# Small reads of two weight matrices at the start of an attention and MoE kernel: 16 partitions in place of 128

## The chip, the cores and the metric

The kernel runs on one core of one Trainium2 chip. The metric is the device time of one execution in microseconds (us): the median of five runs for the kernel before, and comparisons with it for the others. A difference of 0.3% is 0.68 us here.

## The reference

The program computes sliding-window attention with a few sink tokens, and feeds its result through a two-layer network with a gated activation. Cut to what matters:

```python
# q, k, v: (4, 8, 768, 64); n_sink 4, window 128
scores = q @ k.T / sqrt(64)                       # per batch and head
keep = (key < n_sink) | ((0 <= query - key) & (query - key < window))
a = softmax(where(keep, scores, -1e9))
x = (a @ v).transpose(0, 2, 1, 3).reshape(3072, 512)
h = x @ w_in                                      # w_in: (512, 2048)
g = h * sigmoid(beta * h)
out = g @ w_out                                   # w_out: (2048, 512)
```

Inputs and output are float32.

## The kernel before, in words

The 3072 tokens are cut into eight half batches of 384 tokens. For each, the kernel loads q, k and v (lines 613 to 638), casts them to bf16, transposes q and k, computes the scores of blocks of 128 keys by 128 queries that the window touches, takes the exponential on ScalarE, masks, multiplies by v, and normalises. The 384 rows then go through `w_in` (line 910), the gated activation (lines 915 and 917) and `w_out` (line 931). Half batches 0 and 1 are transposed on TensorE (line 697), later ones by DMA transposes (line 734).

`w_in` and `w_out` come in as 16 loads of 512 KB each (`load_w`, lines 640 to 648), float32 into staging tiles `wst` or, for some, into a part of the tile `g` that is not yet in use; they are cast to bf16 by `cast_w`. A load of `w_in` takes 512 columns of 256 rows; a load of `w_out` takes 256 whole rows. On both sides a row index within a block of 128 is the partition.

All of these loads, the transposing DMAs and the stores are issued by SyncE, in one queue. The order of TensorE's work is a string written out by hand (`ORDER`), one letter for each group of matmuls. A planner with a cost for each operation then places the work of the other engines and SyncE's DMAs in time (`schedule`), and puts filler matmuls on a tile of ones where it expects TensorE to be idle during the first 48 us (`fillers`; they have line 1027 in the profile). All this happens when the kernel is built: on the chip each engine runs a fixed list of instructions, with waits on semaphores.

The small reads stand outside of the planner. `G.touch` holds two transfers (line 508), each of which reads four float32 numbers (16 bytes) from the head of many rows: of each of the 512 rows of `w_in`, and of each row in every second block of 128 rows of `w_out`. They land in the tile `seen`, which nothing reads. `emit` issues them on ScalarE's queue ahead of ScalarE's list (lines 385 and 386), and SyncE waits for their semaphore at the very end. The tile `seen` is the last one that is allocated in SBUF. The first instruction of ScalarE's own list is a small exponential that loads its table (line 596).

Of the kernel before, what the change touches and what calls it, by code (L numbers as in the profile page):

```python
# [5 lines left out]
F32 = mybir.dt.float32  # L6
# [10 lines left out]
NM = DF // 128  # L17
# [388 lines left out]
def bass_streamingllm_window__then__act_swish_beta_kernel(  # L406
# [31 lines left out]

    G = Graph()
    _program(nc, G, sb, ps, q, k, v, moe_w_in, moe_w_out, moe_beta, out)  # L440
    G.schedule(ORDER)
    G.resolve()
# [12 lines left out]
def _program(nc, G, sb, ps, q, k, v, w_in, w_out, beta, out):  # L455
# [48 lines left out]
    w_in_src = w_in.rearrange("(c p) f -> p c f", p=128)  # L504
    w_out_src = w_out.rearrange("(m p) n -> p m n", p=128)
    osb = sb("osb", (128, NOUT), F32, NOS)
    seen = sb("seen", (128, 12, 4), F32)
    G.touch = [(seen[:, 0:4, :], w_in_src[:, :, 0:4]), (seen[:, 4:12, :], w_out_src[:, 0:NM:2, 0:4])]
    P = ps("P", (128, 8, 512))

    def add(eng, fn, ns, r=(), w=(), x=(), dma=None, queue=470, ring=64, lag=0, after=()):
# [551 lines left out]
```

The softmax here doesn't subtract the row's maximum and nothing guards it: scores larger than these inputs give would overflow.

## Time and profile before

| What | Before |
|---|---|
| Median of 5 runs | 226.16 us (225.94 to 226.99) |
| The profiled execution | 226.16 us |
| Its span, first to last instruction | 224.4 us |
| Mean granted TensorE clock | 0.992 |
| TensorE busy (share of the span) | 216.1 us (96%) |
| VectorE busy | 141.4 us (63%) |
| ScalarE busy | 141.8 us (63%) |
| GpSimd busy | 67.0 us (30%) |
| DMA moved | 40.95 MB in 104741 packets |
| of it on ScalarE's queue (q10) | 0.02 MB in 1568 packets |

Times in the profile are counted from the first instruction of the program. PE is TensorE's matmuls, PEld its weight loads, DVE VectorE, ACT ScalarE, POOL GpSimd, SP SyncE; a q after an engine's name (SPq, ACTq) means its issuing of DMAs. L697 is line 697 of the kernel. In lists of instructions the columns are start, duration, engine, line, operation, out<-in, and in brackets how long the engine had been idle and what ended that. In tables by stage there are the stage and its length, the busy time of PE, PEld, DVE, ACT and POOL with the number of instructions, the granted TensorE clock, the mean share of the DMA engines that was busy (over 1 where packets overlap), and GB/s. The chain is the work that ended last, followed back from the end: at each step to what released it.

### The profile page before, as it was taken

The numbers are of one execution on the slowest core, as the hardware profiler recorded it, in microseconds if no ns is written. First come the engines' busy times: TensorE is split into PE (matmuls) and PEld (weight loads), VectorE is DVE, ScalarE is ACT, GpSimd is POOL, SyncE is SP. The second block draws the span as 40 slices with busy tenths as digits, with TensorE's granted clock in tenths as the row PEclk, the third lists the DMA queues.
The fourth block names the chain that finished last, engine by engine and source line by source line (L and its number), as shares of the span: only waits on it lengthen the run. The fifth ranks groups of instructions, "written<-read, shape, count | busy, mean of one in ns | idle before, by whom it ended". The sixth has DMA issues, their size and how long they took to land.

```text
span 224.4 us, 4463 instructions
## 1 busy us (share of the span) xinstructions
PE 216.1 (96%) x1699; PEld 120.0 (53%) x1720; DVE 141.4 (63%) x313; ACT 141.8 (63%) x257; POOL 67.0 (30%) x157
## 2 busy tenths in 40 slices
PE   8889999999999999999999999999999999999994
PEld 3446555555455546545554665455555556555443
DVE  1797999788767288839774579657362626455100
ACT  2595998134882877547788748678747756566221
POOL 7274345000362627352109510231436400000000
PEclk9988999999999999999999999999999999999999
DMA  7999989997999999999999999993133033101112
GB/s 160 266 337 374 356 200 352 343 245 138 219 220 213 223 200 243 183 253 219 209 242 180 217 215 236 258 235 96 47 85 82 0 85 83 47 4 47 47 47 93
DMA packets 104741, 40.95 MB, mean 182 GB/s; under 512 B 93312, under 2 KB 97680, under 8 KB 104720
## 3 DMA queue, kind: packets, MB, share of 16 engines
q1 hardware_dynamic: 103152, 40.65, 80.3%
q8 instruction: 13, 0.21, 0.4%
q10 hardware_dynamic: 1568, 0.02, 0.4%
q14 instruction: 8, 0.07, 0.1%
HBM read 27.30 MB, written 6.29 MB: 150 GB/s over the span
## 4 chain that ended last, share of the span: by engine, by line
PE 71%; DVE 10%; DMA 8%; SPq 6%; ACT 3%; issue 1%
PE P L931 31%; PE P L910 28%; DMA v_stage<-in_v_dram 5%; SPq L635 5%; PE P L861 4%; DVE g L917 4%; PE P L783 4%; DMA k_stage<-in_k_dram 3%; PE P L851 2%; DVE k L563 1%; ACT t L915 1%; SPq L891 1%; PE P L819 1%; PE P L1027 1%; DVE w_in L563 1%
## 5 line engine op out<-in xcount | busy, mean ns | idle before, releaser
L910 PE MATMUL P<-xT,w_in 128*128 128x384 bf16 x512 | 92.7, 326 | 0.0
L915 ACT ACTIVATE t<-P,hbeta 128x384 f32<-128x384 f32 x128 | 71.9, 587 | 31.5 <-PE P L910 24.6
L917 DVE SCALAR_TENSOR_TENSOR g<-t,P 128x384 bf16<-128x384 f32 x128 | 68.0, 549 | 35.5 <-ACT t L915 32.9
L931 PE MATMUL P<-w_out,g 128*128 128x512 bf16 (+2 forms) x379 | 88.9, 370 | 1.3 <-ACT t L915 0.2
L798 POOL TENSOR_SCALAR_AFFINE_SELECT E<-E 128x256 bf16<-128x256 bf16 (+1 forms) x109 | 53.0, 518 | 57.1 <-ACT E L792 57.0
L910 PEld LDWEIGHTS P<-xT,w_in 128*128 128x128 bf16 x512 | 48.4, 98 | 34.7 <-issue 0.8
L931 PEld LDWEIGHTS P<-w_out,g 128*128 128x128 bf16 x400 | 36.6, 98 | 36.9 <-issue 1.1
L792 ACT ACTIVATE E<-P 128x768 bf16<-128x768 f32 (+1 forms) x64 | 45.6, 760 | 14.9 <-PE P L783 14.6
L861 PE MATMUL P<-vaug,E 128*128 128x65 bf16 x352 | 19.1, 196 | 0.3 <-DVE vaug L563 0.2
L861 PEld LDWEIGHTS P<-vaug,E 128*128 128x128 bf16 x352 | 17.1, 100 | 3.6 <-ACT E L792 0.7
L558 ACT ACTIVATE osb<-P 128x512 f32<-128x512 f32 (+2 forms) x16 | 9.1, 571 | 15.2 <-PE P L931 15.1
L868 DVE TENSOR_TENSOR onorm<-P,rden 128x384 bf16<-128x384 f32 x32 | 17.5, 553 | 0.5
L783 PE MATMUL P<-qkT 64*128 64x128 bf16 (+1 forms) x256 | 16.7, 242 | 0.9 <-ACT E L792 0.4
L823 ACT ACTIVATE ES<-P 128x128 bf16<-128x128 f32 (+1 forms) x32 | 12.0, 390 | 7.0 <-PE P L819 7.0
L563 DVE CAST k<-k_stage 128x512 bf16<-128x512 f32 (+1 forms) x24 | 11.8, 491 | 5.6 <-DMA k_stage<-in_k_dram 5.6
L783 PEld LDWEIGHTS P<-qkT 64*128 64x128 bf16 x256 | 8.2, 94 | 12.3 <-issue 3.8
L563 DVE CAST q<-q_stage 128x512 bf16<-128x512 f32 (+1 forms) x19 | 9.3, 489 | 6.7 <-DMA q_stage<-in_q_dram 6.5
L851 PE MATMUL P<-vS,ES 128*128 128x130 bf16 x64 | 12.8, 223 | 0.6 <-DVE vS L686 0.4
L563 DVE CAST vaug<-v_stage 128x512 bf16<-128x512 f32 x18 | 8.0, 446 | 7.6 <-DMA v_stage<-in_v_dram 7.5
L725 POOL TENSOR_TENSOR kS<-qkT,headm 128x8 bf16<-128x8 bf16 x16 | 3.0, 212 | 32.6 <-DMA qkT<-k 28.9
L1027 PE MATMUL P<-ones 128*128 128x512 bf16 (+2 forms) x31 | 9.9, 449 | 1.1 <-POOL ones L569 1.1
L809 DVE TENSOR_TENSOR E<-E,maskS 128x512 bf16<-128x512 bf16 x16 | 8.2, 511 | 3.1 <-ACT E L792 3.0
(48 smaller groups left out, 87.9 us busy)
## 6 DMA issues: line engine op xcount, KB each, us to landing
v_stage<-in_v_dram SPq DMA_DIRECT2D x24, 256.0 KB, 4.6
out_dram<-osb SPq DMA_DIRECT2D x23, 256.0 KB, 2.6
q_stage<-in_q_dram SPq DMA_DIRECT2D x18, 256.0 KB, 4.6
k_stage<-in_k_dram SPq DMA_DIRECT2D x18, 256.0 KB, 5.7
wst<-in_moe_w_in_dram SPq DMA_DIRECT2D x5, 512.0 KB, 7.8
wst<-in_moe_w_out_dram SPq DMA_DIRECT2D x4, 512.0 KB, 8.0
g<-in_moe_w_out_dram SPq DMA_DIRECT2D x4, 512.0 KB, 6.8
q_stage<-in_q_dram SPq DMA_DIRECT2D x8, 192.0 KB, 4.6
```

Of the source, the lines that this page charges most:

```text
L563: return lambda e: e.tensor_copy(dst, at())
L783: add("pe", lambda e, dst=dst, own=own, kc=kc, rows=rows, q0=q0, nq=nq: e.matmul(dst(), tokens(own, hp, 1, rows, kc, 1)[:, 0, :], tokens(h ...
L792: add("act", lambda e, src=src, dst_=dst_: e.activation(dst_, src(), AF.Exp, bias=0.0, scale=SCALE), act_ns(256 * n), w=[(k_, z, j) for k_ ...
L798: alts = {"gp": (lambda e, d=d, sg=sg, at_=at_: e.affine_select(d, d, [[0, 2 * len(at_)], [sg, 128]], ALU.is_ge, 0.0, base=min(sg, 0), cha ...
L851: add("pe", lambda e, m=m, o0=o0: e.matmul(A()[:, o0:o0 + 2 * (D + 1)], ES[z][:, (c0 + m) * 128:(c0 + m + 1) * 128], vS[b % 2][:, 2 * hp:2 ...
L861: e.matmul(A()[:, o0:o0 + D + 1], E[z][:, i, hh, :], vaug[vz][:, kb % NK, 2 * hp + hh, :], start=a, stop=o, skip_group_check=True), 39,
L868: add("dve", lambda e: e.tensor_tensor(onorm[:, on, 2 * c0:2 * c1, :], av()[:, :, 0:D], rden[on][:, 0:2 * nb].unsqueeze(2).to_broadcast([1 ...
L910: first = add("pe", lambda e, c=c: e.matmul(hp(), w_in16[:, c, m * 128:(m + 1) * 128], xT[:, hb, c, 128 * c0:128 * c1], start=(c == 0), st ...
L915: add("act", lambda e: e.activation(tt[ti][:, 0:n], hp(), AF.Tanh, bias=0.0, scale=hbeta[:, m:m + 1]), act_ns(n) + 93, r=["hbeta"], w=[("t ...
L917: add("dve", lambda e: e.scalar_tensor_tensor(gt[hb % NG][:, m, 128 * c0:128 * c1], tt[ti][:, 0:n], 1.0, hp(), ALU.add, ALU.mult), dve_ns( ...
L931: add("pe", lambda e, m=m: e.matmul(P[:, bk[0], a:b], gt[hb % NG][:, m, t * 128:(t + 1) * 128], w_out16[:, m, a:b], start=(m == 0), stop=( ...
L1027: G.filler = lambda j, n: lambda e: e.matmul(P[:, j, 0:n].rearrange("p (a b) -> p a b", b=128), ones[:, :], ones[:, :].unsqueeze(1).to_bro ...
```

## The change

The tile `seen` becomes 16 partitions by 20 by 4 numbers. The read of `w_in` takes each eighth row of its four blocks of 128 rows: 64 rows. The read of `w_out` takes each eighth row of all sixteen blocks: 256 rows. Each still reads 16 bytes of a row. Both stay where they were, on ScalarE's queue ahead of its list, and nothing else is different.

```diff
-    seen = sb("seen", (128, 12, 4), F32)
-    G.touch = [(seen[:, 0:4, :], w_in_src[:, :, 0:4]), (seen[:, 4:12, :], w_out_src[:, 0:NM:2, 0:4])]
+    seen = sb("seen", (16, 20, 4), F32)
+    G.touch = [(seen[:, 0:4, :], w_in_src[0:128:8, :, 0:4]),
+               (seen[:, 4:20, :], w_out_src[0:128:8, :, 0:4])]
```

`w_in_src` and `w_out_src` are views of the two matrices with the row in a block as first index and the block as second (lines 504 and 505).

## The prediction

> **What bounds the kernel now.** I read the page's chain first, then the chain in order of time for the first 20 us, since the reads that change are over by 6 us. Shares of the span by engine over the whole chain:
>
> ```profile
> PE 71%; DVE 10%; DMA 8%; SPq 6%; ACT 3%; issue 1%
> ```
>
> TensorE sets most of the end. Not its beginning: there the chain (start, length, what) runs through SyncE's issuing of loads and one load of v.
>
> ```profile
> 5.61 0.87 SPq L635
> ...
> 6.53 5.77 DMA v_stage<-in_v_dram
> ...
> 12.32 0.43 DVE vaug L563
> 12.75 0.33 DVE E L809
> 13.08 0.35 DVE vS L686
> ...
> 13.84 0.23 PE P L851
> ```
>
> SyncE issues loads back to back to 6.5 us, and the third v load, issued last, lands 5.77 us later, because everything ahead of it in the queue must pass first. So up to 12.29 us the bound is how fast the DMA engines empty that queue. Then come VectorE and TensorE, and from 21 to 35 us mostly ScalarE and VectorE. In the piece from 53 to 84 us two more loads are on the chain (k 5.93 us, v 5.29 us); from there on it is matmuls.
>
> Next, what the small reads do to the queue. The DMA queues in the first 12 us (packets, MB, share of the 16 engines' 12 us), with the two issues (KB, us from issue to landing):
>
> ```profile
> q1 hardware_dynamic: 5580, 2.57, 92.0%
> q10 hardware_dynamic: 1568, 0.02, 7.4%
> ...
> seen<-in_moe_w_in_dram ACTq DMA_DIRECT2D x1, 8.0 KB, 3.2
> seen<-in_moe_w_out_dram ACTq DMA_DIRECT2D x1, 16.0 KB, 4.4
> ```
>
> q10 is ScalarE's queue and holds nothing but these reads. Its 1568 packets are 128 x 4 + 128 x 8 = 1536 rows of 16 bytes and 32 completions. They take 7.4% x 12 us = 0.89 us of each engine, or 0.89 x 16 / 1568 = 9.1 ns a packet, for 24 KB. Stage by stage (PE, PEld, DVE, ACT, POOL busy, PEclk, DMA share, GB/s):
>
> ```profile
> 2.50:4.75 2.25, 2.25 (x8) 0.78 (x6) 0.69 (x1) 0.88 (x2) 2.25 (x11) 1.00 1.18 240
> 5.00:6.00 1.00, 0.87 (x7) 0.39 (x5) 0.62 (x2) 0.00 (x0) 0.04 (x1) 1.00 1.11 323
> ```
>
> While the small reads run (1.32 + 4.4 puts the last at 5.7 us) the engines are as busy as after them, but move 240 instead of 323 GB/s.
>
> **The change, part by part.** *Packets.* After it there are 64 + 256 = 320 rows and the same 32 completions: 352 packets, 1216 fewer (78%). Two rows price them. By engine time: 1216 x 9.1 ns / 16 = 0.69 us. By throughput: (323 - 240) GB/s x 2.25 us = 187 KB that didn't move, at 323 GB/s 0.58 us, of which 78% is 0.45 us. From below: nothing, if the engines were short of loads in 2.5 to 4.75 us; their share of 1.18 speaks against that. I take 0.45 us, since the load queue's bytes are what the chain waits for, and keep 0 and 0.69.
>
> *Where that goes.* The v load that lands at 12.29 us lands at about 11.84. TensorE gets k earlier too. Its first transposes end at 5.87 us behind a fixed row of filler matmuls (they hide any gain on q; without them q would gain as well), but then it stands still for k:
>
> ```profile
> PE P L697 <- DVE k L563: 0.9, 1, 0.9
> ```
>
> So 0.9 us of room takes the 0.45. The instructions behind are the same in the same order, hence all after it moves by as much, unless a stage is held by something that doesn't move. From 20 to 35 us VectorE is busy 13.60 of 15 us and ScalarE 13.76; they too begin on earlier data, but fillers[...] and buffers that come free late can eat some. I take 0.05 off: a gain of 0.40 us. The next thing late is the same v load, only less.
>
> *ScalarE's two issues stay, with smaller shapes.*
>
> ```profile
> 0.80 0.49 ACTq L386 DMA_DIRECT2D seen<-in_moe_w_in_dram  x1
> 1.32 0.55 ACTq L386 DMA_DIRECT2D seen<-in_moe_w_out_dram  x1
> 1.90 1.28 ACT L596 ACT_TABLE_LOAD   x1 [1.90 <-issue]
> ...
> 7.58 0.52 ACT L558 ACTIVATE q<-q_stage 128x384 bf16<-128x384 f32 x1 [4.18 <-DMA q_stage<-in_q_dram]
> ```
>
> The nearest row for a plain issue is 0.47 us (SyncE's k loads), so they may shrink from 1.04 to 0.94 us. This is worth nothing: after its warm-up ScalarE idles 4.18 us for q. Were that cover gone, it would be 0.1 us. The queue moves past no other: SyncE issues in parallel, GpSimd has no DMA. The final wait on the reads' semaphore asks for the same count and was over 200 us early. The tile `seen` grows from 192 to 320 bytes a partition and is the last one allocated, so no other tile moves. All nothing.
>
> *What the reads fetch.* Nothing uses `seen`; if the reads matter it is because the later weight loads run faster over places read before. For w_out the places go from every second block of 128 rows (all rows) to every block (each eighth row); for w_in from all rows to each eighth. No wait in the trace shows what that is worth. The nearest row is the start of w_out's loads:
>
> ```profile
> 31.75:32.50 0.75, 0.75 (x8) 0.45 (x6) 0.75 (x3) 0.75 (x3) 0.75 (x2) 1.00 0.68 121
> 32.50:33.25 0.75, 0.75 (x10) 0.57 (x9) 0.75 (x3) 0.75 (x3) 0.05 (x1) 1.00 0.97 341
> ```
>
> At most (341 - 121) / 341 x 0.75 = 0.48 us are lost to a slow start there. That may be odd blocks, never read before; if so, the new form saves it. But the chain from 31 to 54 us holds no DMA, so the saving lies beside VectorE's work: 0. For w_in the bounds are 0 and 0.48 us a load over the first three loads, 1.4 us of loss. Their slack:
>
> ```profile
> 17.37 1.05 POOL L560 TENSOR_SCALAR_AFFINE_SELECT w_in<-wst 128x1024 bf16<-128x1024 f32 x1
> 19.68 1.14 PE L910 MATMUL P<-xT,w_in 128*128 128x384 bf16 x6
> ```
>
> The cast of the second ends at 18.42, 1.26 us before the first matmul that reads w_in. I take 0: w_in's first loads already run at 300 GB/s in 12.75 to 14.0 us against 383 in the next 1.25 us, with every row read before, so the small reads do little for that stage.
>
> [...]
>
> The sum: the profiled execution took 226.16 us (span 224.4, 1.76 around it), equal to the median 226.16. 226.16 - 0.40 = **225.76 us**.
>
> **The rivals.** *Likeliest, 0.58:* the above; 225.4 to 226.2. About 0.06 of it lies past 0.3% (0.68 us), where 0.69 passes whole. One measurement can't tell 0.3% from no change.
>
> *Nothing arrives, 0.15:* the small reads only fill gaps, or the gain ends at the fillers, VectorE or a late buffer: 226.1, 225.8 to 226.5. For it: VectorE and ScalarE are over 90% busy from 20 to 35 us. Against: the chain has no gap in which 0.4 us could vanish.
>
> *A clock step goes too, 0.14:* granted clock by stage:
>
> ```profile
> 4.57:7.98 3.41, 2.50 (x17) 1.24 (x16) 2.33 (x5) 0.40 (x1) 0.47 (x2) 1.00 1.17 287
> ...
> 11.39:14.81 3.42, 2.44 (x32) 1.18 (x31) 2.90 (x10) 3.28 (x7) 2.88 (x8) 1.00 1.07 319
> 14.81:18.22 3.41, 3.41 (x37) 2.38 (x36) 3.04 (x10) 2.32 (x6) 2.34 (x4) 0.50 1.06 376
> ```
>
> [...] Half clock costs at most 3.41 / 2 = 1.7 us, and the 0.76 us of fillers in it are no loss: 0.4 + 0.8 gives 225.0, 224.4 to 225.4. [...]
>
> *Slower, 0.13:* w_in is cold[...]. Each of its first three loads begins 0.48 us late; once their sum passes the 1.26 us of slack, or the cast at 20.60 that already waits 0.35 us for its load is late, TensorE waits. Price 1.0 us net: 227.2; it decides from 1.08 us of added wait (0.40 + 0.68).
>
> **How the numbers follow.** Faster by over 0.3%: 0.06 + 0.14 = 0.20. Slower: 0.13 less 0.01 that ends inside the bound = 0.12. Same: 0.68. The range leaves out half of the clock rival below and half of the slow one above: 225.0 to 227.1; the likeliest's own is 225.4 to 226.2.
>
> **What would show it.** q10 with 352 packets and about 1.7% of the first 12 us; over 290 GB/s in 2.5 to 4.75 us; the third v cast at about 11.9 us; TensorE's wait for k near 0.5 us; matmuls on w_in from about 19.3 us; weights landing no later than before. The prediction is wrong if v lands at 12.3 us as before, if casts of w_in wait over 0.5 us for their loads, or if the half-clock window moves or goes.

## The result: slightly slower, and the profile after

In the first set of runs the changed kernel took 227.14 us in the median of 24 runs, beside 226.56 us for the kernel before (45 runs): a ratio of 1.0031, with a 95% interval of 1.0016 to 1.0045. The ratio uses the fast runs alone (two of the change's, at 229.76 and 230.06 us, are slow), so it is not the quotient of the medians, 1.0026. Two later sets, each beside the kernel before on one chip, gave 1.0010 (0.9993 to 1.0028) and 1.0006 (0.9991 to 1.0020). Weighted by their precision the three make 1.0016, with an interval of about 1.0007 to 1.0025. That takes them as three measures of one thing; they lie further apart than this interval allows, and neither later set shows a loss by itself. So some 0.4 us of loss is the best estimate, where a gain of 0.4 us was forecast, and its size is uncertain. The profiled execution of the first set took 227.71 us, its span was 226.0 us.

The reads did shrink. The DMA queues in the first 12 us, and the two issues, of the changed kernel (packets, MB, share of the engines; KB, us to landing):

```profile
q1 hardware_dynamic: 5654, 2.63, 89.8%
q10 hardware_dynamic: 352, 0.01, 1.6%
...
seen<-in_moe_w_in_dram ACTq DMA_DIRECT2D x1, 1.0 KB, 2.2
seen<-in_moe_w_out_dram ACTq DMA_DIRECT2D x1, 4.0 KB, 2.6
```

q10 went from 1568 packets and 7.4% to 352 and 1.6%, as worked out. The packets beyond the rows, 32 in both, are 16 for each transfer, as many as the program adds to the semaphore for one: with a single transfer of 128 rows there are 144 (e6_k), with three of 512 rows 1584 (e13_thrice). The load queue, q1, even moved a little more in these 12 us, 2.63 MB instead of 2.57. But the loads that are waited for did not come earlier. The third q load is the first to come late, in the repeats of the change too (its cast at 5.93 us in both, 5.73 in the control). The cast before, and with the change:

```profile
5.70 0.42 DVE L563 CAST q<-q_stage 128x384 bf16<-128x384 f32 x1 [0.38 <-DMA q_stage<-in_q_dram]
```

```profile
6.07 0.42 DVE L564 CAST q<-q_stage 128x384 bf16<-128x384 f32 x1 [0.74 <-DMA q_stage<-in_q_dram]
```

An issue of SyncE in front of the v load becomes longer too. The chain before, in a place that the prediction does not show, and then the chain of the changed kernel:

```profile
4.37 0.69 SPq L635
```

```profile
4.39 1.11 SPq L636
...
6.06 0.75 SPq L636
...
6.85 5.70 DMA v_stage<-in_v_dram
...
12.57 0.43 DVE vaug L564
```

The third v load was issued 0.32 us later than before (6.85 against 6.53), and its cast began at 12.57 instead of 12.32 us. Then the two stages of the changed kernel that matter, and the second of them in the kernel before (columns as in the prediction, the last two are DMA share and GB/s):

```profile
2.50:4.75 2.25, 2.25 (x7) 0.76 (x5) 1.03 (x2) 0.73 (x2) 2.25 (x11) 1.00 1.01 274
12.00:15.00 3.00, 1.78 (x26) 0.89 (x26) 2.55 (x7) 2.67 (x6) 2.40 (x7) 1.00 0.90 249
```

```profile
12.00:15.00 3.00, 2.07 (x27) 1.18 (x27) 2.64 (x8) 2.86 (x6) 2.39 (x6) 0.97 1.05 334
```

In 2.5 to 4.75 us the rate rose from 240 to 274 GB/s, but 2.0 to 2.5 us fell from 157 to 93, and 5 to 6 us from 323 to 290: by 6 us both kernels had moved 1.00 MB of loads. And in 12 to 15 us, where the first loads of `w_in` pass, it fell from 334 to 249 GB/s, 8 us after the last small read of the changed kernel landed (1.28 + 2.6 us). In two repeats of the change this rate was 306 and 316, so the size of that fall is not to be relied on; the share fell each time (0.90, 0.94 and 0.97). What comes of it on GpSimd and TensorE, first before (its matmul is in the prediction), then with the change:

```profile
15.31 1.05 POOL L560 TENSOR_SCALAR_AFFINE_SELECT w_in<-wst 128x1024 bf16<-128x1024 f32 x1 [0.43 <-DMA wst<-in_moe_w_in_dram]
...
17.01 0.41 POOL L798 TENSOR_SCALAR_AFFINE_SELECT E<-E 128x256 bf16<-128x256 bf16 x1 [0.65 <-ACT E L792]
```

```profile
16.46 1.10 POOL L561 TENSOR_SCALAR_AFFINE_SELECT w_in<-wst 128x1024 bf16<-128x1024 f32 x1 [1.49 <-DMA wst<-in_moe_w_in_dram]
...
17.93 1.04 POOL L561 TENSOR_SCALAR_AFFINE_SELECT w_in<-wst 128x1024 bf16<-128x1024 f32 x1
...
20.25 1.14 PE L911 MATMUL P<-xT,w_in 128*128 128x384 bf16 x6
```

The first cast of `w_in` waits 1.49 us for its load and begins at 16.46 us (before: 0.43 us, 15.31). The first matmul on `w_in` begins at 20.25 instead of 19.68 us, 0.57 us later.

The same matmul can be compared in both traces, all 512 of this line in order. The delay stays at 0.56 us up to 56 us, is 0.76 us from 99 to 137 us, and 1.53 us from 151 us to the end. That last step is not the change's: two executions of the kernel before (the control below) differ by 0.18 us up to 56 us, by 0.64 us from 99 to 137 and by 1.05 us from 151 us. One profile's span is therefore no measure here. What reproduces is the part up to 56 us: the first matmul on `w_in` comes at 20.12 and 20.08 us in the repeats of the change, and at 19.87 us in the control.

### The profile page after: what moved, and what is told of

Same layout as the page of the kernel before. It is cut to its first block, busy times and chain, and to the rows that moved or that the text cites. A ratio compares the mean times of both kernels' runs of the same rounds, so it can differ in the third digit from the quotient of the medians.

```text
span 226.0 us, 4463 instructions
## 1 busy us (share of the span) xinstructions
PE 216.8 (96%) x1699; PEld 119.5 (53%) x1720; DVE 142.1 (63%) x313; ACT 141.9 (63%) x257; POOL 66.3 (29%) x157
## 3 DMA queue, kind: packets, MB, share of 16 engines
HBM read 27.28 MB, written 6.29 MB: 149 GB/s over the span
## 4 chain that ended last, share of the span: by engine, by line
PE 58%; DMA 14%; DVE 13%; SPq 10%; ACT 2%; issue 1%
PE P L932 27%; PE P L911 23%; DMA v_stage<-in_v_dram 9%; SPq L636 7%; DVE g L918 5%; PE P L862 3%; PE P L784 3%; SPq L892 2%; DMA k_stage<-in_k_dram 2%; DMA out_dram<-osb 2%; DMA q_stage<-in_q_dram 2%; DVE onorm L869 2%; ACT t L916 1%; DVE vaug L564 1%; PE P L852 1%
## 5 line engine op out<-in xcount | busy, mean ns | idle before, releaser
L799 POOL TENSOR_SCALAR_AFFINE_SELECT E<-E 128x256 bf16<-128x256 bf16 (+1 forms) x109 | 52.4, 512 | 57.1 <-ACT E L793 57.0
L862 PE MATMUL P<-vaug,E 128*128 128x65 bf16 x352 | 18.6, 193 | 0.7 <-DVE E L804 0.4
L862 PEld LDWEIGHTS P<-vaug,E 128*128 128x128 bf16 x352 | 16.5, 97 | 3.9 <-ACT E L793 0.7
L564 DVE CAST q<-q_stage 128x512 bf16<-128x512 f32 (+1 forms) x19 | 9.9, 524 | 7.6 <-DMA q_stage<-in_q_dram 7.4
L1028 PE MATMUL P<-ones 128*128 128x512 bf16 (+2 forms) x31 | 10.6, 474 | 1.2 <-POOL ones L570 1.1
L565 DVE TENSOR_SCALAR osb<-P 128x512 f32<-128x512 f32 x9 | 6.2, 691 | 5.6 <-DMA out_dram<-osb 2.6
```

Of the source, the lines that this page charges most:

```text
L564: return lambda e: e.tensor_copy(dst, at())
L799: alts = {"gp": (lambda e, d=d, sg=sg, at_=at_: e.affine_select(d, d, [[0, 2 * len(at_)], [sg, 128]], ALU.is_ge, 0.0, base=min(sg, 0), cha ...
L862: e.matmul(A()[:, o0:o0 + D + 1], E[z][:, i, hh, :], vaug[vz][:, kb % NK, 2 * hp + hh, :], start=a, stop=o, skip_group_check=True), 39,
```

## The experiments

Each run was timed in five rounds beside the kernel before. The table gathers what the profiles and times say. "v3" and "w_in" are the starts of the third v cast and of the first `w_in` cast, "matmul" that of the first matmul on `w_in`, in us; "12 to 15" is the DMA share and GB/s in that stage.

| Run | small reads | q10 packets | v3 | w_in | matmul | 12 to 15 | ratio (95%) |
|---|---|---|---|---|---|---|---|
| before | 128 partitions | 1568 | 12.32 | 15.31 | 19.68 | 1.05, 334 | 1 |
| e8_before | same | 1568 | 12.34 | 15.29 | 19.87 | 1.05, 339 | 0.9998 (0.9984 to 1.0013) |
| the change | 16 partitions | 352 | 12.57 | 16.46 | 20.25 | 0.90, 249 | 1.0031 (1.0016 to 1.0045) |
| e7_after | same | 352 | 12.43 | 16.23 | 20.12 | 0.94, 306 | 1.0010 (0.9993 to 1.0028) |
| e16_after | same | 352 | 12.65 | 16.31 | 20.08 | 0.97, 316 | 1.0006 (0.9991 to 1.0020) |
| e1_none | none | 0 | 12.70 | 16.14 | 20.09 | 0.95, 294 | 0.9997 (0.9973 to 1.0022) |
| e2_match | 16, rows 32 to 92 | 352 | 12.47 | 16.04 | 19.95 | 0.99, 330 | 1.0003 (0.9985 to 1.0021) |
| e3_shift | 16, rows 36 to 96 | 352 | 12.46 | 16.00 | 20.14 | 0.95, 320 | 1.0004 (0.9986 to 1.0021) |
| e4_win_full | w_in 128, w_out 16 | 800 | 12.53 | 16.17 | 20.08 | 0.93, 281 | 1.0011 (0.9990 to 1.0032) |
| e5_wout_full | w_in 16, w_out 128 | 1120 | 12.55 | 16.24 | 20.19 | 0.93, 249 | 1.0005 (0.9990 to 1.0021) |
| e6_k | 16, of k | 144 | 12.73 | 16.57 | 20.63 | 0.84, 249 | 1.0002 (0.9982 to 1.0023) |
| e11_elsewhere | 128, of q | 1568 | 12.20 | 15.07 | 19.36 | 1.06, 346 | 0.9992 (0.9971 to 1.0013) |
| e17_elsewhere | same | 1568 | 12.26 | 15.26 | 19.65 | 1.05, 332 | 1.0004 (0.9991 to 1.0017) |
| e13_thrice | 128, w_in thrice | 1584 | 12.36 | 15.26 | 20.05 | 1.05, 337 | 1.0011 (0.9986 to 1.0036) |
| e10_more | 128, more of w_out | 2592 | 13.07 | 16.98 | 19.36 | 1.05, 310 | 1.0030 (1.0013 to 1.0047) |
| e12_half | 64 partitions | 800 | 12.88 | 17.04 | 19.36 | 0.85, 269 | 1.0026 (1.0012 to 1.0041) |
| e14_16part | 16, of q, 96 each | 1568 | 12.89 | 16.36 | 20.32 | 1.08, 303 | 1.0029 (1.0014 to 1.0045) |
| e15_128few | 128, of q, 3 each | 416 | 12.68 | 15.78 | 19.92 | 0.95, 299 | 1.0015 (0.9998 to 1.0031) |

The edits below are against the changed kernel; `seen` fits the shape of the reads each time.

### No small reads, and other rows in 16 partitions

```diff
-    G.touch = [(seen[:, 0:4, :], w_in_src[0:128:8, :, 0:4]), ...
+    G.touch = []                                    # e1_none; the last wait for them goes too
+    ... w_in_src[32:96:4, :, 0:4], w_out_src[32:96:4, :, 0:4]     # e2_match
+    ... w_in_src[36:100:4, :, 0:4], w_out_src[36:100:4, :, 0:4]   # e3_shift
```

> No small reads at all (and no wait for them at the end). Theory A, w_in is cold: the small reads pay by making the first loads of w_in fast, so without them the first cast of w_in on GpSimd starts at 16.5 us or later (15.3 before, 16.5 with the change) and the time is 227.1 to 228.5. Theory B, a crowded start: the change loses because its small reads reach the DMA engines ahead of the first packets of q and stall them, so without any the third v cast starts near 11.9 us and the time is 226.1 or less.

> 16 partitions as in the change, but rows 32, 36, ... 92 of each block[...]. Theory A1, warmth belongs to an engine: first cast of w_in near 15.3 us, time like before, 226.6 within 0.3. Theory A2, warmth belongs to addresses alone: rows 0 to 31 and 96 to 127 were never near a read, the time is like the change, 227.1. Theory B: like the change, 227.1, as the packets at the start are the same in number.

> 16 partitions, rows 36, 40, ... 96 of each block: the same addresses as in the run with rows 32 to 92 but for the ends[...]. Theory A1, engine: first cast of w_in near 16.5 us, 227.1 or more. Theories A2 and B: the same as the run with rows 32 to 92 within 0.2 us.

Without any small reads the stage that the forecast priced looks like this:

```profile
2.50:4.75 2.25, 2.25 (x7) 0.76 (x5) 0.98 (x2) 0.00 (x0) 2.25 (x11) 1.00 0.91 253
12.00:15.00 3.00, 2.07 (x28) 0.99 (x27) 2.62 (x8) 2.96 (x6) 2.45 (x8) 1.00 0.95 294
```

With nothing beside the loads they still run at only 253 GB/s, with the engines at 0.91 where they had been at 1.18, and the third v cast comes at 12.70 us: 0.38 us later than with 1568 small reads. So most of the shortfall against 323 GB/s was not made by the small reads. Theory B fails: its 11.9 us is missed by 0.8. Theory A's cast is late, at 16.14 us, though not at 16.5, and its time does not come: 0.9997 against the 1.002 to 1.009 that 227.1 to 228.5 would be, with an interval that just reaches 1.0022.

The two forms of 16 rows were to part theory A1 from A2. Which engine reads which row is not shown: no trace here names it. First rows 32 to 92, then rows 36 to 96:

```profile
16.04 1.05 POOL L561 TENSOR_SCALAR_AFFINE_SELECT w_in<-wst 128x1024 bf16<-128x1024 f32 x1 [1.15 <-DMA wst<-in_moe_w_in_dram]
```

```profile
16.00 1.05 POOL L561 TENSOR_SCALAR_AFFINE_SELECT w_in<-wst 128x1024 bf16<-128x1024 f32 x1 [1.19 <-DMA wst<-in_moe_w_in_dram]
```

They agree to 0.04 us, where theory A1 expected casts near 15.3 us for the first and near 16.5 us for the second. Its forecasts failed; whether an engine plays a part stays open.

### One half of the change at a time, the control, and k

```diff
+    (seen[:, 0:4, :], w_in_src[:, :, 0:4]), (seen[0:16, 4:20, :], w_out_src[0:128:8, :, 0:4])       # e4_win_full
+    (seen[0:16, 0:4, :], w_in_src[0:128:8, :, 0:4]), (seen[:, 4:12, :], w_out_src[:, 0:NM:2, 0:4])  # e5_wout_full
+    k[0, :, 0:HALF, :].rearrange("h (p j) d -> p h (j d)", j=NB // 2)[0:128:8, :, 0:4]              # e6_k, alone
```

> w_in as before (128 partitions, 512 rows), w_out as in the change (16 partitions, 256 rows). Theory A: the loss is w_in's, so the time is that of before, 226.6 within 0.3, first cast of w_in near 15.3 us. Theory B: w_out's small reads are as in the change and w_in's bring more packets, so no better than the change, 227.1.

> w_in as in the change (16 partitions), w_out as before (128 partitions, every second block), the other half of the split. Theory A: all of the loss is w_in's, 1.003, w_in cast near 16.5 us. Theory C: within 0.998 to 1.002.

> The kernel before once more, under a name of its own, as the measure of what two equal programs differ by. Every theory: ratio 1.000, and its distance from 1 says how far the other ratios of this chip can be trusted; the third v cast and the first w_in cast of its profile say how much these move from execution to execution.

> The change once more, beside its rivals on one chip. Theory A, w_in is cold: ratio 1.003 (227.2 against 226.6) and the first w_in cast near 16.5 us. Theory C, the small reads do next to nothing for the end: ratio within 0.998 to 1.002, as without any small reads (0.9997).

> No small reads of the weights; in their place small reads of k, each eighth row of the first half batch in eight heads, 16 bytes each (16 partitions, 128 rows). Theory D, the load queue stands still by itself at 3.5 to 5 us, because the first packets of k meet cold rows (117 to 250 GB/s there with no small reads at all): read early, k runs on, over 300 GB/s in 3.5 to 5 us, the third v cast is 0.3 to 0.5 us earlier than the 12.70 us without small reads, and the time falls by as much, 226.2 where before has 226.6. If the stall is not k's coldness: as without small reads, 253 GB/s in 2.5 to 4.75 us.

The first half was to settle it for theory A, and did not: with all 512 rows of `w_in` read just as before, its first cast still comes at 16.17 us. With `w_out` as before and `w_in` as in the change it comes at 16.24. Only both together gave 15.3. The control says how far that can be trusted: a second execution of the kernel before has its casts at 12.34 and 15.29 us, within 0.02 us of the first, and its ratio is 0.9998. The change's repeat has 16.23 us against 16.46. So the gap of about 1 us between the two kernels is real. The repeat's ratio, 1.0010, lies where theory C has it. Small reads of k changed nothing for the better: 184 GB/s in 3.5 to 5 us and v3 at 12.73. That this slow stage is k's coldness was the expectation, and it fell.

### Elsewhere, thrice, more, half

```diff
+    q[3, 0:4, HALF:S, :].rearrange("h (p j) d -> p h (j d)", j=NB // 2)[:, :, 0:4]  # e11, e17: 128 x 4 rows of q
+    q[3, 0:8, HALF:S, :] ...                                                       # and 128 x 8, both in place of the weights
+    w_in_src[:, :, 0:4], w_in_src[:, :, 4:8], w_in_src[:, :, 8:12]                 # e13_thrice
+    w_in_src[:, :, 0:4], w_out_src[:, :, 0:4]                                      # e10_more
+    w_in_src[0:128:2, :, 0:4], w_out_src[0:128:2, 0:NM:2, 0:4]                     # e12_half
```

> As many small reads as before (1536 of 16 bytes, 128 partitions), but of q of the last batch in place of the weights. Theory E, addresses: what helps the first w_in loads is that the weights' rows were read, so they are late as without small reads: first w_in cast at 16.0 us or later, ratio 1.001 to 1.003. Theory F, the number of packets: 1568 packets at the start change how the loads' packets lie in time, wherever they point, so the first w_in cast is near 15.3 us and the ratio 0.999 to 1.001.

> All 512 rows of w_in read three times over (columns 0 to 3, 4 to 7, 8 to 11: 1536 small reads, as many as before), none of w_out. Theory E1, w_in's own rows read often or late enough: first w_in cast near 15.3 us. Theory E2, w_out's reads are needed too: 16.0 us or later, as where w_out had 256 rows. Theory F: near 15.3 us.

> 128 partitions for both, and all sixteen blocks of w_out: 2560 small reads, 1024 more than before. Theory F and E2: first w_in cast at 15.3 us or a little earlier; against it 1024 packets of 9.1 ns on 16 engines, 0.58 us, if they cost their time: third v cast at 12.3 us if they lie in a stall that is there anyway, 12.9 us if they cost. Ratio 0.999 to 1.001 or 1.002 to 1.003.

> 64 partitions: every second row of w_in's four blocks and of w_out's even blocks, 768 small reads. Theory E: half of the rows warm half of what 128 do, first w_in cast between 15.3 and 16.3 us. Theory F: also between. If the cast is at 15.3 us, a row in two is enough for the weights' first loads and the packets' number doesn't matter; ratio 1.000 then, else 1.001 to 1.002.

This decides against the addresses. 1536 small reads of q of the last batch, which has nothing to do with these loads, bring back the early cast. The stage and the cast of that run:

```profile
12.00:15.00 3.00, 2.10 (x32) 1.23 (x32) 2.75 (x9) 2.88 (x6) 2.26 (x6) 1.00 1.06 346
```

```profile
15.07 1.08 POOL L561 TENSOR_SCALAR_AFFINE_SELECT w_in<-wst 128x1024 bf16<-128x1024 f32 x1 [0.31 <-DMA wst<-in_moe_w_in_dram]
```

346 GB/s, the cast at 15.07 us, a ratio of 0.9992, and no row of a weight was read early. Three times the rows of `w_in` alone did the same (15.26). But more is not better: 1024 more reads moved v3 by 0.75 us to 13.07, and the cast to 16.98, where 15.3 or earlier was expected. The 0.58 us of their engine time is near the 0.75, so here the packets may have cost their time; it is not shown, as 64 partitions with 800 packets have v3 at 12.88 too. They also have the latest cast, 17.04 us, which no theory had.

### Number or shape, on one chip with the change

```diff
+    q[3].rearrange("h s d -> (h s) d").rearrange("(p r) d -> p r d", p=16)[:, 0:32, 0:2]   # e14_16part
+    ... [:, 32:96, 0:2]                                                                    # 16 x 96 reads in all
+    q[3, 0:1, ...][:, :, 0:4], q[3, 0:2, ...][:, :, 0:4]                                   # e15_128few: 128 x 3, rows as in e11
```

> 1536 small reads as before, but of q of the last batch, 8 bytes each, and into 16 partitions as in the change (96 rows on each). Theory G, the number of packets: first w_in cast near 15.2 us, DMA share in 12 to 15 us over 1.0, ratio 0.999 to 1.001. Theory H, the shape: it takes 128 partitions, so here as with the change, w_in cast at 16.0 us or later, share under 1.0.

> 384 small reads of q of the last batch (the change has 320), 16 bytes each, into 128 partitions as before (3 rows on each). Theory G, the number: as with the change, first w_in cast at 16.0 us or later, ratio 1.001 to 1.003. Theory H, the shape: near 15.2 us, ratio 0.999 to 1.001.

> The change once more, on the chip of the two runs that part number and shape. If the early delay is what costs: w_in cast at 16.0 to 16.5 us and a ratio of 1.001 to 1.003; a ratio of 1.000 would say that the loss isn't tied to it.

> The 1536 small reads of q of the last batch once more, beside the change on one chip: w_in cast near 15.1 us, ratio 0.999 to 1.000, and faster than the change by 0.2% or more, if the early delay reaches the end.

Neither alone is enough. 1536 reads in 16 partitions: 16.36 us, and the slowest of these four (1.0029); they were of 8 bytes, a second difference. 384 reads in 128 partitions: 15.78 us, between. 1536 in 128 partitions: 15.26. So neither theory G nor theory H came true as a whole in either run. And the last expectation fell: with casts 1 us apart, the reads of q (1.0004) and the change (1.0006) end alike on this chip, where 0.2% was expected. That the early delay reaches the end is therefore not shown.

Number has a mark of its own, though: with 1568 packets or more the DMA share in 12 to 15 us was 1.05 to 1.08 in all seven runs, with fewer 0.84 to 0.99 in all eleven. A mean share under 1 leaves part of the engines' time unused, while the first load of `w_in`, issued at 10.52 us in the changed kernel, lands only at about 16.4 us. Which engines stood idle, and why a thousand packets several microseconds earlier prevent it, stays open: the records at hand do not name the engine.

How the late load reaches the first matmul on `w_in` can be read from VectorE's masks, which wait beside a cast on GpSimd. The kernel before and the changed one, on VectorE:

```profile
15.75 0.88 DVE L809 TENSOR_TENSOR E<-E,maskS 128x512 bf16<-128x512 bf16 x1
...
16.66 0.25 DVE L803 TENSOR_TENSOR E<-E,maskT 128x256 bf16<-128x256 bf16 x1
...
17.86 0.70 DVE L803 TENSOR_TENSOR E<-E,maskT 128x256 bf16<-128x256 bf16 x1
```

```profile
16.25 0.41 DVE L810 TENSOR_TENSOR E<-E,maskS 128x512 bf16<-128x512 bf16 x1
...
16.68 1.02 DVE L804 TENSOR_TENSOR E<-E,maskT 128x256 bf16<-128x256 bf16 x1
...
18.20 0.92 DVE L804 TENSOR_TENSOR E<-E,maskT 128x256 bf16<-128x256 bf16 x1
```

Before, the first cast (15.31 to 16.36 us) lies over the first of these masks; with the change it begins at 16.46 and lies over the second, which takes 1.02 us instead of 0.25. The third mask meets the second cast in both kernels and ends just after it. This meeting sets the matmul: in all 18 executions of the table the last mask ends 0.14 us after a cast on GpSimd, and the first matmul on `w_in` begins 1.13 us after the mask. The second cast ends at 18.42 us before and at 18.97 with the change, as GpSimd had idled 0.65 us between the casts, which took up the rest of the 1.15 us; the matmul follows at 19.68 and 20.25. In two runs, e10_more and e12_half, the meeting is with the first cast (in e12_half it runs from 17.04 to 18.09 us, the mask ends at 18.23, the matmul begins at 19.36). There the latest first cast goes with the earliest matmul, and still with ratios of 1.0030 and 1.0026. So neither the cast nor this matmul ranks the ends of the runs. In the changed kernel the chain runs over VectorE from 12.57 to 19.59 us; its start, the third v cast, brings 0.25 us of delay of its own. I tested the masks' part by taking the weights' casts off GpSimd, in both kernels:

```diff
-        any_of(copies(dst, src_, {"act": 947, "dve": 602, "gp": 1060}), r=[("wst", j % NWS)], w=[("w16", m, h)])
+        any_of(copies(dst, src_, {"act": 947, "dve": 602}), r=[("wst", j % NWS)], w=[("w16", m, h)])
```

> The kernel before, with the weight casts taken from GpSimd's choices: the planner gives them to VectorE and ScalarE, and places the work around them anew. Theory J: between 15 and 19 us the end is set by VectorE's masks, which take 0.9 to 1.0 us beside a cast on GpSimd and 0.25 alone (two such meetings, 1.4 us); without the casts there, the first matmul on w_in comes 0.3 to 0.8 us earlier than 19.7 and the ratio is 0.997 to 0.999, less what the casts cost VectorE (0.69 us each). Theory K: VectorE is full there and takes the casts' 1.4 us in place of the slow masks: ratio 1.000 to 1.004.

> The change with the weight casts taken from GpSimd in the same way. If the late first load of w_in reaches the end only through GpSimd's cast and the masks beside it, this and the last run are equal within 0.1%; if a late w_in costs on VectorE too (its cast then stands in VectorE's order and waits there), this one is slower by 0.2 to 0.5%.

The masks then took 0.27 and 0.28 us, and the first matmul on `w_in` came at 18.44 us, 1.24 us earlier:

```profile
18.44 1.14 PE L910 MATMUL P<-xT,w_in 128*128 128x384 bf16 x6
```

Yet both kernels lost 2.3% (1.0234, 1.0205 to 1.0262, and 1.0235, 1.0195 to 1.0274): the planner places all later work anew too, and by 40 us the lead was gone, by 151 us it was a lag of 4.93 us. So the masks' wait for the casts is shown, and that it sets the first matmul. How that reaches the end is not: between these two kernels the matmul's delay is 0.33 us at first, of which 0.25 us is there at the third v cast (12.41 and 12.66), and 1.0 us a few us later, with no cast of weights on GpSimd, while their times agree, within an interval too wide to say more. Theories J and K both missed the end.

## Why the prediction was wrong

- **The packets' price, the step that failed.** "By throughput: (323 - 240) GB/s x 2.25 us = 187 KB that didn't move" took the difference between two stages for the work of what lay in the first. With no small reads the same stage runs at 253 GB/s. The step behind it failed as well, that "the load queue's bytes are what the chain waits for": q1 moved as much by 6 us and 0.06 MB more by 12 us, and yet the third q cast came 0.37 us later and the third v cast at 12.57 instead of 11.9 us, 0.25 us later than before. That the loads land in the order of their issue is in the trace: of the eleven up to the third v load, nine have a cast that waited for its load, and these nine, from 3.76 to 12.32 us before, follow that order. That the small reads' bytes and packets set when a load lands is not. The engine time of 0.69 us was right as engine time (7.4% to 1.6%), but it did not become time won. The lower bound of nothing, set aside because of the share of 1.18, was nearer than the 0.45 us taken, and still too high. Why the third q load comes later with the change (and later still, its cast at 6.22 us, with no small reads) stays open.
- **The room of 0.9 us on TensorE.** It did not serve. In the profiled execution the wait for k was gone because TensorE came to it later, and k later too (its cast at 6.61 instead of 6.29 us): fillers followed each other every 0.43 us up to 6.15 us, before only up to 4.45 us and then every 0.21, and the transposes of q began at 6.47 instead of 5.54 us. The room was partly luck of that execution: in the control they began at 6.03 us.
- **ScalarE's issues.** 0.44 us each against 0.49 and 0.55, table load at 1.75 instead of 1.90 us, worth nothing: right.
- **What the reads fetch: nothing.** Right about the addresses, by the runs elsewhere. But the conclusion that only the queue's time was left to count was wrong. The first load of `w_in`, some 6 to 10 us later, depends on the number and shape of what went before, a term that the sum did not have.
- **The slow rival.** It named the right place (the first load of `w_in`, its cast, the first matmul behind) and the wrong cause: with no row of a weight read early the cast came at 15.07 and 15.26 us (e11_elsewhere, e17_elsewhere), and rows 32 to 92 and 36 to 96 in 16 partitions give 16.04 and 16.00 us. The slack was misread as well. The 1.26 us from the second cast's end to the matmul was no slack but a fixed run of work (0.14 us to the mask's end, 1.13 us from there to the matmul): it is 1.26 to 1.28 us in all 18 executions, counted from the cast that the mask meets. The slack was GpSimd's idle time between the two casts, 0.65 us of it before, which is why a delay of 1.15 us at the first cast gave only 0.57 us at the matmul.
- **The clock rival.** The half-clock window from 14.81 to 18.22 us (clock 0.50) is in one execution of the kernel before and absent in the other (1.00 there; mean clock 0.992 and 1.000); of the change's three it is in one (0.53 in that stage of e7_after). What brings it is not shown. That a shift of 0.4 us takes it away was only an estimate of mine from the work in the stage ahead, and the control speaks against it: there the stage from 11.39 to 14.81 us had even less work on TensorE, 2.19 us against 2.44, and the clock was 1.00 in it and in the next. For the first matmul on `w_in` the window is worth nothing: without it 19.87, with it 19.68 us, both 1.13 us after the mask, although with it the profile draws the chain over TensorE from 13.84 us. The 0.8 us of the rival does not follow from its terms either: 1.7 us less half of the 0.76 us of fillers is 1.3.
- **What was to show it.** 352 packets and 1.6% came true. Over 290 GB/s in 2.5 to 4.75 us (274), v at 11.9 us (12.57), a wait for k near 0.5 us (none), matmuls on `w_in` from 19.3 us (20.25) and weights no later (1.15 us later) did not. Of its signs of being wrong, a cast of `w_in` that waits over 0.5 us for its load came true (1.49 us).
- **The size.** The chance of 0.12 for slower by over 0.3% had a part in it, and 227.14 us lies 0.04 us beyond the range. Of the 1.38 us between 225.76 and 227.14, 0.40 us is the kernel before itself (226.56 us in this set, 226.16 when the prediction was made), 0.40 us the gain that did not come, and 0.58 us the loss. So it was chance on which side of the range's end the time fell; the sign of the change was forecast wrong. Three sets together put the loss at 0.16%, inside the bound that was called the same, but on the other side of zero. "Nothing arrives" was the nearest rival.

## What to carry to other kernels

A stage that moves fewer bytes while something else runs is no proof that the something else takes the difference (here 240 GB/s with it, 253 without): run it once without, before pricing its removal. Bytes moved are not loads landed: here the queue had moved more by 12 us (2.63 against 2.57 MB) and the load that was waited for came later (cast at 12.57 against 12.32 us). Small transfers at the start moved loads several microseconds later (over their forms the first cast of `w_in` began at 15.07 to 17.04 us), for a reason that these records do not give, so their number and form have to be measured and not argued. The time between two instructions is slack only if nothing fixed lies in it: the 1.26 us here stayed the same, within 0.02 us, in every execution. And before a single profile's span is read, profile the same kernel twice: here equal programs differ by about 1 us at the end, while the start agrees within 0.02 us on a cast.

## What the runs showed that I had not expected

- 1536 reads of 16 bytes each into 128 partitions, of data that nobody uses, bring the first cast of `w_in` about 1 us earlier (15.1 to 15.3 us in five executions, 15.8 to 17.0 us in the thirteen others).
- Number and spread both matter: 1536 reads in 128 partitions 15.26 us, 1536 in 16 partitions 16.36, 384 in 128 partitions 15.78.
- VectorE's mask of 128 x 256 takes 0.25 us alone; when it meets a cast of 128 x 1024 on GpSimd it ends about 0.14 us after the cast, and took up to 1.16 us.
- A first matmul on `w_in` 1.24 us earlier ended 2.3% later, under another order of the work behind it.
